# Sink products of two head pairs side by side at half depth, and a new order of the later steps, in a fused attention and gated-MLP kernel

## The chip, the cores and the metric

The kernel runs on one core of a Trainium2 chip. The core has five engines that work at the same time: TensorE (PE, with its weight loads shown as PEld) for matrix products, VectorE (DVE), ScalarE (ACT), GpSimd (POOL), and SyncE (SP), which here issues DMA transfers. Engines wait for one another through semaphores. The metric is the device time of one execution in microseconds; the median of several runs is compared.

## The reference, cut to what matters

```python
def _attn_ref(q, k, v, n_sink, window):          # q, k, v: 4 batches, 8 heads, 768 positions, 64
    scores = np.matmul(q, k.transpose(0, 1, 3, 2)) / np.sqrt(D)
    keep = (pos[None, :] < 4) | in_window         # 4 sink keys, and the last 128 keys
    a = softmax(np.where(keep, scores, -1e9))
    return np.matmul(a, v)

def _moe_ref(x, w_in, g_ln, w_sg, b_sg, w_out):   # x: 4, 768, 512
    u, v = np.split(gelu(x @ w_in), 2, axis=-1)
    v_n = (v - mean) / np.sqrt(var + 1e-6) * g_ln
    v_s = np.einsum('ts,bsd->btd', w_sg, v_n) + b_sg[None, :, None]
    return x + (u * v_s) @ w_out
```

The attention's output, heads laid side by side, is the `x` of the second function.

## The kernel before

The kernel is a list of steps, `STEPS`, written out by hand or by a planner outside the kernel. A loop runs over the list and calls, for each step, the function of that name with the numbers behind it; a last letter A, D or P chooses ScalarE, VectorE or GpSimd. Each engine carries out its own steps in the order of the list. Nothing reorders them. A step on one engine waits only for the steps whose results, or whose freed buffers, it needs.

The numbers are the batch b (0 to 3), then a head pair p (0 to 3; two heads fill 128 partitions), a pair of 128-row token tiles g (0 to 2), a half of the tokens, or a token tile.

- Loads: `LQ.b.i`, `LK.b.i` (a tile of q or k), `LVH.b.i` (v of four heads), `LW`, `LWS`, `LWO`, `LB` (weights). All are issued by POOL, and at most eight are under way: the ninth waits, in POOL's queue, for the first to land.
- Turning q and k so that the head dimension lies on partitions: `TQ`, `TK` on PE and their copies `EQ`, `EK` for batches 0 to 2, DMA transposes `DQ`, `DK` from SP for batch 3.
- Scores: `QK.b.p.g` (PE, two heads on rows 0-63 and 64-127 of the array), `EX` (exponential, ACT), `MK` (window mask: one multiplication on DVE, or two selects on POOL).
- Sink scores of all heads at once: `KS` (DVE), `SK` (PE), `SX` (ACT). They lie in `exs`, 32 partitions for each head pair, so pairs 0 and 1 fill partitions 0-63 and pairs 2 and 3 fill 64-127. `VSM.b` (DVE) makes `v_sink`, the sink rows of v, zero outside each head's own partitions.
- `AV.b.p.k` (PE): products with v for half k of the tokens (three token tiles in batches 1 to 3). For each tile and head one or two products of 65 columns (lines 524 and 528), then for tiles from the third on one sink product of 130 columns over all 128 partitions of `exs` (line 531). `NR` (DVE) divides by the sum and writes `x_sb`.
- Turning x: `XT`/`XE` in batch 0, in the others a DMA transpose `XD.b.half` from SP.
- MLP: `MV`/`GV` (the v half of x @ w_in on PE, gelu on ACT), `BN` (statistics, DVE), `RS` (reciprocal root, POOL), `NM` (DVE), `Z` (normalised v, ACT or DVE); `MU`/`GU` (the u half); `WT`/`WE` turn w_sg once; `SP.b.half.dc` (PE, product with w_sg over all six z tiles of the batch), `GT` (DVE), `GM` (times u, DVE or POOL), `OU.b.t` (PE, output product), `RA` (adds x, DVE), `ST` (store, SP). `OH`, `RH`, `SH` are the same in halves of the columns for the last tile.
- `HM.n` puts n products on a zero tile in front of the next product that takes a fresh buffer. `TBL` touches ACT with an exponential or a gelu.

What couples the engines are rings of buffers: `fresh(ring, key)` takes the next tile of a ring and so waits until the tile's last reader is done. PSUM holds two score tiles (`sc`, for `QK`, `MV`, `MU`) and four others (`mm`, for transposes, `SK`, `AV`, `SP`, `OU`). Ten tiles `P` hold exponentials.

The steps before and after one another in the list are on purpose a mixture of batches: the MLP of batch b runs between the attention steps of batch b+1.

Of the kernel before, what the change touches and what calls it, by code (L numbers as in the profile page):

```python
# [25 lines left out]
MK.0.1.0.D SX.0.1 SX.0.2 QK.0.3.1 MK.0.2.1.P GCP.D NR.0.0.0 EX.0.3.0 AV.0.0.1 AV.0.1.0 AV.0.1.1 NR.0.0.1 EX.0.3.1
QK.0.1.2 NR.0.1.0 AV.0.2.0 AV.0.3.0 EX.0.1.2 MK.0.3.1.P NR.0.1.1 QK.0.2.2 AV.0.2.1 NR.0.2.0 EX.0.2.2 TQ.1.0 NR.0.3.0
MK.0.1.2.P QK.0.3.2 AV.0.3.1 EQ.1.0.A NR.0.2.1 XT.0.0 NR.0.3.1 LWS.0 AV.0.0.2 EX.0.3.2 TBL.G AV.0.1.2 XE.0.0.D LK.1.1
XT.0.1 MK.0.2.2.D MV.0.0 XE.0.1.A LK.1.2 NR.0.0.2 MK.0.3.2.D LK.1.3 NR.0.1.2 AV.0.2.2 AV.0.3.2 LQ.1.2 NR.0.2.2 GV.0.0
MV.0.1 NR.0.3.2 LQ.1.3 BN.0.0 LWS.1 XT.0.2 GV.0.1 MU.0.1 XE.0.2.A BN.0.1 WT.0 GU.0.1 TK.1.0 MV.0.2 RS.0.1 EK.1.0.A  # L30
LK.1.4 NM.0.1 WE.0.A WT.1 GV.0.2 LK.1.5 TK.1.1 MU.0.2 LB.P EK.1.1.A BN.0.2 Z.0.0.A LK.2.0 WT.2 GU.0.2 MU.0.0 WE.1.D
RS.0.2 WE.2.D Z.0.1.A LQ.2.0 NM.0.2 Z.0.2.A Z.0.3.D Z.0.4.D WT.3 LQ.2.1 WT.4 GU.0.0 TBL.E WE.3.D WT.5 LQ.1.4 Z.0.5.D
TQ.1.1 QK.1.0.0 EQ.1.1.D QK.1.1.0 LQ.1.5 SP.0.0.0 WE.4.D LK.2.1 EX.1.0.0 VSM.1 SP.0.0.1 WE.5.D EX.1.1.0 LVH.1.0
GT.0.0.0 TK.1.2 KS.1 GT.0.0.1 QK.1.2.0 QK.1.3.0 EX.1.2.0 SP.0.0.2 LVH.1.1 GM.0.0.0.D EX.1.3.0 MK.1.2.0.D TQ.2.0
EK.1.2.A LQ.2.2 QK.1.0.1 EQ.2.0.D QK.1.1.1 TQ.1.2 EX.1.0.1 GT.0.0.2 LWO SP.0.0.3 EQ.1.2.D EX.1.1.1 LK.2.2 MK.1.0.1.D
TK.2.0 MK.1.0.0.D QK.1.2.1 LK.2.3 EK.2.0.A QK.1.3.1 MK.1.3.0.D SK.1.0 GM.0.0.1.D LQ.2.3 SP.0.1.0 EX.1.2.1 GT.0.0.3
MK.1.1.0.D LQ.2.4 EX.1.3.1 SP.0.1.1 MK.1.1.1.D LQ.2.5 MK.1.2.1.D SX.1.0 QK.1.0.2 QK.1.1.2 GT.0.1.0 EX.1.0.2 GM.0.0.2.P
SP.0.1.2 GT.0.1.1 EX.1.1.2 LK.2.4 GM.0.1.0.D AV.1.0.0 MK.1.3.1.D AV.1.1.0 LK.2.5 GM.0.0.3.D QK.1.2.2 GT.0.1.2 QK.1.3.2
EX.1.2.2 SP.0.1.3 NR.1.0.0 MK.1.1.2.P EX.1.3.2 NR.1.1.0 AV.1.2.0 AV.1.3.0 MK.1.0.2.P GT.0.1.3 QK.2.0.0 QK.2.1.0
NR.1.2.0 EX.2.0.0 OU.0.0 MK.1.2.2.P NR.1.3.0 TK.2.1 RA.0.0 AV.1.0.1 XD.1.0 EK.2.1.A MK.1.3.2.P AV.1.1.1 NR.1.0.1  # L40
AV.1.2.1 EX.2.1.0 GM.0.1.2.P NR.1.1.1 AV.1.3.1 NR.1.2.1 QK.2.2.0 LK.3.0 QK.2.3.0 EX.2.2.0 OU.0.1 NR.1.3.1 GM.0.1.3.P
EX.2.3.0 TBL.G OU.0.2 XD.1.1 RA.0.1 GM.0.1.1.P TK.2.2 MK.2.3.0.D TQ.2.1 LVH.2.0 TQ.2.2 EQ.2.1.D MV.1.0 EQ.2.2.D LQ.3.0
EK.2.2.D LQ.3.1 VSM.2 MU.1.0 GV.1.0 MK.2.1.0.D LVH.2.1 BN.1.0 MV.1.1 GU.1.0 LQ.3.2 RA.0.2 LQ.3.3 MK.2.0.0.D MV.1.2
GV.1.1 MK.2.2.0.D LK.3.1 KS.2 LK.3.2 BN.1.1 MU.1.1 GV.1.2 LK.3.3 BN.1.2 RS.1.1 MU.1.2 GU.1.1 LQ.3.4 NM.1.1 Z.1.0.A
RS.1.2 OU.0.3 GU.1.2 TBL.E LQ.3.5 NM.1.2 Z.1.1.D SK.2.0 Z.1.4.D QK.2.0.1 Z.1.2.D Z.1.3.A QK.2.1.1 Z.1.5.D OU.0.4
# [5 lines left out]
AV.2.2.1 GM.1.1.3.P ST.0.1 NR.2.1.1 AV.2.3.1 ST.0.2 ST.0.5 GM.1.1.0.P SK.3.0 NR.2.2.1 QK.3.2.0 QK.3.3.0 NR.2.3.1
EX.3.2.0 GM.1.1.2.P SP.1.0.2 EX.3.3.0 XD.2.1 SP.1.0.3 GT.1.0.2 SX.3.0 TBL.G MK.3.3.0.D MV.2.0 GM.1.0.2.P DK.3.1
GM.1.1.1.D LK.3.4 MK.3.0.0.D OU.1.3 LVH.3.0 GV.2.0 OU.1.4 RA.1.3 LVH.3.1 OU.1.5 ST.1.3 RA.1.4 GT.1.0.3 MV.2.1 ST.1.4
MK.3.1.0.D LK.3.5 BN.2.0 GM.1.0.3.P MV.2.2 GV.2.1 BN.2.1 MU.2.1 GV.2.2 BN.2.2 RS.2.1 MU.2.0 GU.2.1 NM.2.1 RA.1.5
RS.2.2 MU.2.2 GU.2.0 NM.2.2 Z.2.4.D Z.2.5.D Z.2.0.A Z.2.1.D OU.1.0 GU.2.2 TBL.E Z.2.2.D MK.3.2.0.D OU.1.1 RA.1.0
Z.2.3.D QK.3.0.1 QK.3.1.1 RA.1.1 SP.2.0.0 EX.3.0.1 DK.3.2 EX.3.1.1 OU.1.2 MK.3.0.1.P GT.2.0.0 ST.1.5 VSM.3 ST.1.0
QK.3.2.1 ST.1.1 QK.3.3.1 EX.3.2.1 SP.2.1.0 GM.2.0.0.D MK.3.1.1.P RA.1.2 EX.3.3.1 SP.2.0.1 ST.1.2 MK.3.3.1.P QK.3.0.2
GT.2.0.1 QK.3.1.2 EX.3.0.2 SP.2.1.1 GT.2.1.0 MK.3.2.1.P EX.3.1.2 GM.2.1.0.D SP.2.1.2 GT.2.1.1 GM.2.0.1.D AV.3.0.0
MK.3.1.2.P GT.2.1.2 AV.3.1.0 NR.3.0.0 AV.3.2.0 AV.3.3.0 MK.3.0.2.P NR.3.1.0 QK.3.2.2 QK.3.3.2 EX.3.2.2 SP.2.0.2
NR.3.2.0 NR.3.3.0 EX.3.3.2 TBL.G SP.2.0.3 MK.3.2.2.P GT.2.0.2 XD.3.0 AV.3.0.1 GT.2.0.3 MK.3.3.2.P AV.3.1.1 NR.3.0.1  # L60
# [16 lines left out]
def kernel(  # L77
# [412 lines left out]
    def MK(b, p, g, e="D"):  # L490
        w = wide(g)
        pt = P[b, p, g]
        if e == "D":
# [4 lines left out]
        nc.gpsimd.affine_select(out=p4[:, :, :, 0:128], in_=p4[:, :, :, 0:128], compare_op=ALU.is_ge,  # L498
                                fill=0.0, base=0, pattern=[[0, 2], [0, 2], [1, 128]],
                                channel_multiplier=-1)  # L500
        nc.gpsimd.affine_select(out=p4[:, :, :, 128:256], in_=p4[:, :, :, 128:256],  # L501
                                compare_op=ALU.is_ge, fill=0.0, base=-1,
                                pattern=[[0, 2], [0, 2], [-1, 128]], channel_multiplier=1)
# [7 lines left out]

    def AV(b, p, k):
        vb = v_sb[b]
        fresh(mm_ring, ("a", b, p, k))
        av = av_view(b, p, k)
        i0, n = rowsof(b, k)
        first = True
        for il in range(n):
            i = i0 + il
            for hl in range(2):  # L520
# [5 lines left out]
                if i >= 1:  # L526
                    c = 128 if i % 2 else 384
                    nc.tensor.matmul(av[:, il, hl, :], pt[:, hl, c:c + 128], vb[:, h, i - 1, :],  # L528
                                     start=False, stop=(i < 2 and il == n - 1 and hl == 1))
# [186 lines left out]
```

## Time and profile before

| | |
|---|---|
| runs of the kernel before | median 155.58 us of 3 (155.23 to 155.91) |
| the profiled execution | 155.89 us, of which the span of instructions is 154.2 us |
| instructions | 3867 |
| DVE, ACT, POOL busy | 122.9, 100.0, 99.7 us |
| DMA | 24.67 MB in 87178 packets |

The profile is one execution. Its page gives busy time by engine, the span in 40 slices, and the chain of waits that ended last. The timeline lists instructions in order of time, those of one kind merged, with an idle time in brackets where the engine stood, and what ended it. Shapes are partitions x elements; `64*128` in front of a product is the part of the array that it uses (rows * columns). Times within a row are microseconds from the span's start. Durations of products overlap, since they are pipelined.

### The profile page before, as it was taken

To read this page: it belongs to the slowest core of one execution; us is meant where nothing else is said; L and a number is where in the kernel's file an instruction comes from. 1 tells how busy PE (TensorE), PEld (TensorE's weight loads), DVE (VectorE), ACT (ScalarE), POOL (GpSimd) and SP (SyncE) were. 2 spreads that over 40 slices of the span, in tenths; PEclk is the share of its full clock that TensorE was granted. 3 is DMA by queue.
4 is the path that set the end of the run, shared out by engine and by line. 5 is a ranking of instruction groups with operands and counts; after the bars stand their busy time and mean duration, and the time that the engine had idled before them with its cause. 6 is when DMAs were issued, how large, how long until landed. Compare 5 with 4: busy or idle time off the path is not lost.

```text
span 154.2 us, 3867 instructions
## 1 busy us (share of the span) xinstructions
PE 145.7 (95%) x1540; PEld 94.5 (61%) x1554; DVE 122.9 (80%) x296; ACT 100.0 (65%) x117; POOL 99.7 (65%) x127
## 2 busy tenths in 40 slices
...
PEclk9999999999999999999999999999999999999999
...
DMA packets 87178, 24.67 MB, mean 160 GB/s; under 512 B 78772, under 2 KB 84920, under 8 KB 87160
## 3 DMA queue, kind: packets, MB, share of 16 engines
...
q8 instruction: 12, 0.20, 0.5%
q14 instruction: 6, 0.05, 0.1%
...
## 4 chain that ended last, share of the span: by engine, by line
PE 54%; POOL 18%; DMA 15%; ACT 4%; DVE 4%; issue 2%; SPq 1%; DVEq 0%; ACTq 0%; POOLq 0%
PE mm L627 15%; DMA v_sb<-in_v_dram 11%; PE mm L644 10%; PE sc L566 9%; PE sc L607 8%; POOL q L225 5%; POOL k L225 4%; DMA uT<-in_k_dram 4%; PE sc L483 4%; PE mm L524 3%; POOL v_sb L271 3%; PE mm L528 2%; POOL wsg_gated L637 2%; POOL P L498 2%; POOL P L501 2%
## 5 line engine op out<-in xcount | busy, mean ns | idle before, releaser
L488 ACT ACTIVATE P<-sc 128x1024 bf16<-128x1024 f32 (+1 forms) x48 | 43.4, 952 | 10.3 <-PE sc L483 10.1
L627 PE MATMUL mm<-wsgT,z 128*128 128x384 bf16 x192 | 34.4, 327 | 0.3 <-ACT z L597 0.3
L627 PEld LDWEIGHTS <-z 128*128 128x128 bf16 x192 | 17.6, 98 | 12.5 <-issue 0.7
L570 ACT ACTIVATE vt<-sc 128x1024 f32<-128x1024 f32 x12 | 12.3, 1027 | 18.4 <-PE sc L566 18.4
L632 DVE SCALAR_TENSOR_TENSOR gtmp<-mm,g_sb,b_bc 128x384 bf16<-128x384 f32 x32 | 19.0, 610 | 4.2 <-PE mm L627 4.0
L637 POOL TENSOR_TENSOR wsg_gated<-gtmp,uT 128x384 bf16<-128x384 bf16 x15 | 14.9, 1006 | 11.3 <-DVE gtmp L632 11.2
L607 PE MATMUL sc<-xT,w_in_sb 128*128 128x256 bf16 x192 | 22.1, 273 | 0.0
L566 PE MATMUL sc<-w_in_sb,xT 128*128 128x512 bf16 x92 | 21.8, 379 | 0.2
L644 PE MATMUL mm<-w_out_sb,wsg_gated 128*128 128x512 bf16 x85 | 21.2, 379 | 0.5
L498 POOL TENSOR_SCALAR_AFFINE_SELECT P<-P 128x512 bf16<-128x512 bf16 x21 | 13.7, 653 | 11.4 <-ACT P L488 11.4
L607 PEld LDWEIGHTS <-w_in_sb 128*128 128x128 bf16 x192 | 18.7, 98 | 2.9
L579 DVE BATCH_NORM_STATS2 st<-vt 128x6 f32<-128x512 f32 x24 | 15.4, 685 | 6.1 <-ACT vt L570 6.0
L541 DVE TENSOR_TENSOR x_sb<-mm,rcp 128x384 bf16<-128x384 f32 (+1 forms) x36 | 18.5, 513 | 1.2
L588 POOL TENSOR_TENSOR rs<-rs,neg_half 128x4 f32<-128x4 f32 (+1 forms) x8 | 7.1, 882 | 15.8 <-DVE rs L583 14.4
L225 POOL DMA_DIRECT2D k<-in_k_dram x18 | 16.4, 924 | 1.3 <-DMA v_sb<-in_v_dram 1.3
L648 DVE TENSOR_TENSOR ot<-mm,x_sb 128x512 f32<-128x512 f32 x23 | 15.4, 683 | 2.2 <-PE mm L644 2.2
L225 POOL DMA_DIRECT2D q<-in_q_dram x18 | 16.8, 956 | 0.0
L524 PE MATMUL mm<-v_sb,P 128*128 128x65 bf16 x192 | 16.1, 194 | 0.6 <-DVE x_sb L541 0.4
L524 PEld LDWEIGHTS <-P 128*128 128x128 bf16 x192 | 14.5, 97 | 2.5 <-DMA v_sb<-in_v_dram 0.6
L528 PE MATMUL mm<-v_sb,P 128*128 128x65 bf16 x160 | 15.4, 193 | 0.4 <-POOL P L501 0.4
L612 ACT ACTIVATE uT<-sc 128x1024 bf16<-128x1024 f32 x12 | 12.2, 1024 | 5.1 <-PE sc L607 5.1
L566 PEld LDWEIGHTS <-xT 128*128 128x128 bf16 x96 | 9.2, 98 | 10.1
...
## 6 DMA issues: line engine op xcount, KB each, us to landing
...
```

Source lines behind the costliest of these rows:

```text
L225: return nc.gpsimd.dma_start(out=dst.rearrange("p (h d) -> p h d", h=H), in_=heads(src, b, i))
L488: nc.scalar.activation(out=P.new((b, p, g))[:, :, 0:w], in_=sc_ring[b, p, g][:, :, 0:w], func=AF.Exp, scale=scale)
L498: nc.gpsimd.affine_select(out=p4[:, :, :, 0:128], in_=p4[:, :, :, 0:128], compare_op=ALU.is_ge, fill=0.0, base=0, pattern=[[0, 2], [0, 2], ...
L524: nc.tensor.matmul(av[:, il, hl, :], pt[:, hl, c:c + 128], vb[:, h, i, :], start=first, stop=False)
L528: nc.tensor.matmul(av[:, il, hl, :], pt[:, hl, c:c + 128], vb[:, h, i - 1, :], start=False, stop=(i < 2 and il == n - 1 and hl == 1))
L541: nc.vector.tensor_mul(x_sb.get(b)[:, i0:i0 + n, 128 * p:128 * (p + 1)].rearrange("p t (h d) -> p t h d", h=2), av[:, :, :, 0:Dh], rcp[:, ...
L566: nc.tensor.matmul(hp[:, jl, :], xT[b][:, 2 * g + jl, c, :], w_in_sb[:, c, d_half:2 * d_half], start=(c == 0), stop=(c == KD - 1))
L607: nc.tensor.matmul(hp[:, dc // 2, 256 * (dc % 2):256 * (dc % 2 + 1)], w_in_sb[:, c, 128 * dc:128 * (dc + 1)], xT[b][:, 2 * g:2 * g + 2, c, :],
L627: nc.tensor.matmul(ps[:, 0:NH], z[b][:, si, 128 * dc:128 * (dc + 1)], wsgT[:, si, NH * hf:NH * (hf + 1)], start=(si == 0), stop=(si == NT ...
L632: nc.vector.scalar_tensor_tensor(out=gtmp.new((b, hf, dc)), in0=mm_ring["g", b, hf, dc][:, 0:NH], scalar=g_sb[:, dc:dc + 1], in1=b_bc[:, N ...
L637: (nc.vector if e == "D" else nc.gpsimd).tensor_mul(gated(b, hf)[:, dc, :], gtmp[b, hf, dc], uT[b][:, dc, NH * hf:NH * (hf + 1)])
L644: nc.tensor.matmul(ps, gated(b, hf)[:, dc, 128 * tl:128 * (tl + 1)], w_out_sb[:, dc, :], start=(dc == 0), stop=(dc == KU - 1))
```

## The change

In batches 1 and 2, for the second half of the tokens, `AV` no longer issues its sink products. A new step `SN.b.p0.k` issues them for head pairs p0 and p0 + 2 together, ahead of their `AV`: for each of the three token tiles one product on partitions 0-63 (pair p0) and one on 64-127 (pair p0 + 2), each into its own accumulator. `SN` takes both `mm` tiles, opens the accumulation, and `AV` adds to it. Batches 0 and 3 keep the old products.

The first 145 steps of the list that issue work stay as they are. (Steps `MK...N` are new in the list there and issue nothing.) From then on the list is in another order: the score steps `QK` stand in other pairs and more often alone; some copies, masks, multiplications and `Z` steps change between ACT, DVE and POOL; loads stand at other places among POOL's masks; `HM.2` and `HM.1` are new in front of `WT.2` and `WT.3`; `TBL` steps stand elsewhere, and two more of them end the list's ACT part.

```diff
+    def split(b, k):
+        return k == 1 and b in (1, 2)
+
+    def SN(b, p0, k):
+        i0, n = rowsof(b, k)
+        for p in (p0, p0 + 2):
+            fresh(mm_ring, ("a", b, p, k))
+        for il in range(n):
+            for p in (p0, p0 + 2):
+                rows = slice(64 * (p // 2), 64 * (p // 2) + 64)
+                nc.tensor.matmul(av_view(b, p, k)[:, il, :, :].rearrange("p h d -> p (h d)"),
+                                 exs[b][rows, 128 * (i0 + il - 2):128 * (i0 + il - 1)],
+                                 v_sink[b][rows, 2 * p:2 * p + 2, :].rearrange("p h d -> p (h d)"),
+                                 start=(il == 0), stop=False)
+
     def AV(b, p, k):
         vb = v_sb[b]
-        fresh(mm_ring, ("a", b, p, k))
+        if not split(b, k):
+            fresh(mm_ring, ("a", b, p, k))
...
-        first = True
+        first = not split(b, k)
...
-                                     start=False, stop=(i < 2 and il == n - 1 and hl == 1))
-            if i >= 2:
+                                     start=False,
+                                     stop=((i < 2 or split(b, k)) and il == n - 1 and hl == 1))
+            if i >= 2 and not split(b, k):
...
```

The list from the place where the orders part up to batch 1's `MV.1.0`, before:

```text
LK.1.4 NM.0.1 WE.0.A WT.1 GV.0.2 LK.1.5 TK.1.1 MU.0.2 LB.P EK.1.1.A BN.0.2 Z.0.0.A LK.2.0 WT.2 GU.0.2 MU.0.0 WE.1.D
RS.0.2 WE.2.D Z.0.1.A LQ.2.0 NM.0.2 Z.0.2.A Z.0.3.D Z.0.4.D WT.3 LQ.2.1 WT.4 GU.0.0 TBL.E WE.3.D WT.5 LQ.1.4 Z.0.5.D
TQ.1.1 QK.1.0.0 EQ.1.1.D QK.1.1.0 LQ.1.5 SP.0.0.0 WE.4.D LK.2.1 EX.1.0.0 VSM.1 SP.0.0.1 WE.5.D EX.1.1.0 LVH.1.0
...
SP.0.1.2 GT.0.1.1 EX.1.1.2 LK.2.4 GM.0.1.0.D AV.1.0.0 MK.1.3.1.D AV.1.1.0 LK.2.5 GM.0.0.3.D QK.1.2.2 GT.0.1.2 QK.1.3.2
EX.1.2.2 SP.0.1.3 NR.1.0.0 MK.1.1.2.P EX.1.3.2 NR.1.1.0 AV.1.2.0 AV.1.3.0 MK.1.0.2.P GT.0.1.3 QK.2.0.0 QK.2.1.0
NR.1.2.0 EX.2.0.0 OU.0.0 MK.1.2.2.P NR.1.3.0 TK.2.1 RA.0.0 AV.1.0.1 XD.1.0 EK.2.1.A MK.1.3.2.P AV.1.1.1 NR.1.0.1
AV.1.2.1 EX.2.1.0 GM.0.1.2.P NR.1.1.1 AV.1.3.1 NR.1.2.1 QK.2.2.0 LK.3.0 QK.2.3.0 EX.2.2.0 OU.0.1 NR.1.3.1 GM.0.1.3.P
EX.2.3.0 TBL.G OU.0.2 XD.1.1 RA.0.1 GM.0.1.1.P TK.2.2 MK.2.3.0.D TQ.2.1 LVH.2.0 TQ.2.2 EQ.2.1.D MV.1.0
```

and after:

```text
LK.1.4 MU.0.2 RS.0.1 LK.1.5 WE.0.A HM.2 WT.2 LB.P NM.0.1 EK.1.0.A GV.0.2 Z.0.2.D GU.0.2 LK.2.0
BN.0.2 LQ.2.0 Z.0.1.D TK.1.1 TQ.1.1 RS.0.2 EK.1.1.D LQ.2.1 Z.0.0.A Z.0.3.A MU.0.0 WT.1 WE.2.D WT.4 NM.0.2 Z.0.4.A KS.1
EQ.1.1.D WE.1.D WT.5 Z.0.5.D WE.4.D TK.1.2 WE.5.D VSM.1 LQ.1.4 QK.1.1.0 EK.1.2.D GU.0.0 LQ.1.5 EX.1.1.0 QK.1.0.0
...
SP.0.1.3 EX.1.3.1 EK.2.0.D QK.1.2.2 QK.1.1.2 MK.1.2.1.D GT.0.1.3 MK.1.0.1.P AV.1.0.0 GM.0.0.3.P LQ.2.4 GT.0.1.0 LQ.2.5
NR.1.0.0 LK.2.4 SP.0.1.2 MK.1.3.1.P EX.1.2.2 LK.2.5 AV.1.2.0 MK.1.2.2.P QK.1.3.2 MK.1.0.2.D AV.1.3.0 EX.1.1.2 GT.0.1.2
QK.2.1.0 EX.1.3.2 EX.2.1.0 OU.0.0 MK.1.3.2.P NR.1.2.0 TK.2.1 QK.2.0.0 NR.1.3.0 MK.1.1.2.P SN.1.0.1 RA.0.0 AV.1.0.1
TQ.2.1 XD.1.0 EK.2.1.A AV.1.2.1 QK.2.3.0 NR.1.0.1 SN.1.1.1 NR.1.2.1 EQ.2.1.A EX.2.0.0 AV.1.1.1 AV.1.3.1 OU.0.1
QK.2.2.0 TQ.2.2 LK.3.0 NR.1.1.1 GM.0.1.3.P NR.1.3.1 GM.0.1.2.P EX.2.3.0 TK.2.2 OU.0.2 RA.0.1 MV.1.0
```

Around batch 1's second product with w_sg and batch 2's attention, after:

```text
BN.1.2 LQ.3.4 GU.1.1 OU.0.4 OU.0.3 NM.1.1 Z.1.2.D LQ.3.5 QK.2.0.1 Z.1.1.A Z.1.3.D RS.1.2 RA.0.4 Z.1.0.D GU.1.2 EX.2.0.1 NM.1.2
Z.1.4.D Z.1.5.D QK.2.1.1 EX.2.1.1 DK.3.0 SK.2.0 RA.0.3 SP.1.1.0
...
QK.2.3.2 QK.2.2.2 OU.0.5 EX.2.2.2 SP.1.1.3 MK.2.1.2.P RA.0.5 EX.2.3.2 ST.0.4 SN.2.0.1 QK.3.1.0 XD.2.0 QK.3.0.0
GT.1.1.3 EX.3.1.0 ST.0.1 AV.2.0.1 MK.2.2.2.P AV.2.2.1 ST.0.2 SN.2.1.1 MK.2.3.2.P QK.3.3.0 NR.2.0.1 AV.2.1.1
...
OU.1.3 GT.1.0.2 KS.3 GM.1.0.2.P XD.2.1 DK.3.1 SK.3.0 MK.3.3.0.D SX.3.0 LK.3.4 QK.3.2.0 LVH.3.0 LVH.3.1 EX.3.2.0 MV.2.0
```

More of the change, by code (lines that the diff above doesn't have):

```diff
@@ L26 @@
[L26 to L45, printed above, removed]
@@ L51 @@
[L51 to L60, printed above, removed]
@@ new lines @@
+LQ.3.2 EK.2.2.A MV.1.1 MK.2.2.0.D MV.1.2 MK.2.1.0.D GV.1.1 LQ.3.3 LK.3.1 KS.2 TBL.G.2 LK.3.2 LK.3.3 BN.1.0 GV.1.2
+MU.1.1 GM.0.1.0.D BN.1.1 RS.1.1 MU.1.2 BN.1.2 LQ.3.4 GU.1.1 OU.0.4 OU.0.3 NM.1.1 Z.1.2.D LQ.3.5 QK.2.0.1 Z.1.1.A
+Z.1.3.D RS.1.2 RA.0.4 Z.1.0.D GU.1.2 EX.2.0.1 NM.1.2 Z.1.4.D Z.1.5.D QK.2.1.1 EX.2.1.1 DK.3.0 SK.2.0 RA.0.3 SP.1.1.0
+SP.1.0.1 QK.2.3.1 SX.2.0 GT.1.1.0 QK.2.2.1 GM.1.1.0.D MK.2.0.1.D EX.2.2.1 DQ.3.0 MK.2.1.1.P ST.0.3 EX.2.3.1 GT.1.0.1
+MK.2.2.1.P SP.1.1.2 DQ.3.1 MK.2.3.1.P SP.1.0.0 GM.1.0.1.D AV.2.0.0 QK.2.1.2 QK.2.0.2 GT.1.1.2 NR.2.0.0 GT.1.0.0
```

68 lines of the change are left out of this document (48 added, 20 removed).

## The prediction

> **What bounds the kernel now.** I read the page first, then TensorE's timeline step by step, then the waits that the timeline names.
>
> ```profile
> span 154.2 us, 3867 instructions
> ...
> PE 145.7 (95%) x1540; PEld 94.5 (61%) x1554; DVE 122.9 (80%) x296; ACT 100.0 (65%) x117; POOL 99.7 (65%) x127
> ...
> PEclk9999999999999999999999999999999999999999
> ...
> PE 54%; POOL 18%; DMA 15%; ACT 4%; DVE 4%; issue 2%; SPq 1%; DVEq 0%; ACTq 0%; POOLq 0%
> ```
>
> TensorE (PE) is busy for 95% of the span at the full granted clock, and the chain that ended last runs through it more than through anything else. So a product costs its place in line: the distance from its start to the start of the next step. I therefore price by starts, not by durations. In the timeline below the columns are start, duration, engine, line, operation, operands, shapes and count:
>
> ```profile
> 32.32 0.50 PE L619 MATMUL mm<-iden,wsg_gated 128*128 128x128 bf16 x6
> ...
> 37.93 0.61 PE L382 MATMUL mm<-iden,q 128*128 128x128 bf16 x8
> 38.48 0.50 PE L483 MATMUL sc<-qT,kT 64*128 64x256 bf16 x8
> 38.91 2.12 PE L627 MATMUL mm<-wsgT,z 128*128 128x384 bf16 x12
> 40.87 0.61 PE L382 MATMUL mm<-iden,k 128*128 128x128 bf16 x8
> ...
> 48.84 0.61 PE L483 MATMUL sc<-qT,kT 64*128 64x256 bf16 x12
> 49.38 1.15 PE L627 MATMUL mm<-wsgT,z 128*128 128x384 bf16 x6
> ...
> 61.11 0.61 PE L382 MATMUL mm<-iden,k 128*128 128x128 bf16 x8
> 61.56 1.06 PE L382 MATMUL mm<-iden,q 128*128 128x128 bf16 x16
> 62.45 1.89 PE L566 MATMUL sc<-w_in_sb,xT 128*128 128x512 bf16 x8
> 64.18 1.91 PE L607 MATMUL sc<-xT,w_in_sb 128*128 128x256 bf16 x16
> ```
>
> Three prices come out. Eight transposes followed by more of their kind take 61.56 - 61.11 = 0.45 us; in front of score products (64 rows) the same eight take 38.48 - 37.93 = 0.55. So **entering half-depth work costs 0.10**. The two score steps at 48.84 stream 2 x (2 x 256 + 4 x 128) = 2048 columns and take 0.54. At L627's pace (12 x 384 columns in 1.96 us) these would take 0.87 one after the other, and half of that side by side: 0.44, plus **0.10 for leaving**. So products on rows 0-63 and 64-127 overlap here. And a 512-column product costs (64.18 - 62.45) / 8 = 0.216.
>
> TensorE does stop in a few places:
>
> ```profile
> 53.54 0.50 PE L483 MATMUL sc<-qT,kT 64*128 64x256 bf16 x8
> ...
> 55.07 0.39 PE L382 MATMUL mm<-iden,k 128*128 128x128 bf16 x4
> 55.83 0.40 PE L382 MATMUL mm<-iden,k 128*128 128x128 bf16 x4 [0.37 <-DMA k<-in_k_dram]
> 56.06 0.19 PE L524 MATMUL mm<-v_sb,P 128*128 128x65 bf16 x1
> ...
> 57.92 0.20 PE L524 MATMUL mm<-v_sb,P 128*128 128x65 bf16 x1
> 58.51 0.20 PE L528 MATMUL mm<-v_sb,P 128*128 128x65 bf16 x1 [0.39 <-POOL P L501]
> ...
> 75.65 0.76 PE L627 MATMUL mm<-wsgT,z 128*128 128x384 bf16 x3
> 76.67 1.15 PE L627 MATMUL mm<-wsgT,z 128*128 128x384 bf16 x6 [0.26 <-ACT z L597]
> ...
> 88.06 0.22 PE L531 MATMUL mm<-v_sink,exs 128*128 128x130 bf16 x1
> 88.34 0.20 PE L524 MATMUL mm<-v_sb,P 128*128 128x65 bf16 x1
> ```
>
> Measured against the prices: from 53.54 to 55.07 stand 0.43 of scores and 0.86 of OU.0.0 (four 512-column products), so 0.24 is lost; TK.2.1 takes 0.99 for 0.45, 0.54 lost; AV.1.3.1 stands 0.59 - 0.03 = 0.56 for a Pool mask; SP.1.0.0 needs 0.49 for three products and takes 1.02, 0.53 lost on z; the gap after 88.06 is 0.28 for 0.06, 0.22 lost. Together **2.1 us** of waiting between 32.3 us and the end. That is all a new order can take away from TensorE, and the work it adds must come out of it.
>
> **The change, part by part.**
>
> *Sink products.* In batches 1 and 2, 24 full-depth products of 130 columns go; 24 half-depth ones in 12 side-by-side pairs come.
>
> ```profile
> 25.84 0.22 PE L531 MATMUL mm<-v_sink,exs 128*128 128x130 bf16 x1
> 25.89 0.38 PE L566 MATMUL sc<-w_in_sb,xT 128*128 128x512 bf16 x1
> ...
> L531 PEld LDWEIGHTS <-exs 128*128 128x128 bf16 x64 | 6.2, 98 | 0.0
> ```
>
> A full one costs 0.05 to 0.06. No row shows a half-depth sink pair. Below, it cannot be cheaper than one such product (0.06); above, two weight loads one after the other, 0.196. I take 0.06, since the score products (other weights for each, same 64 rows) do overlap. 24 x 0.06 - 12 x 0.06 = **-0.7 us**. SN holds two accumulators at once, so it waits for two NR steps; behind it on TensorE wait the AV products and the next scores. By my count the later NR ends 0.1 to 0.6 before.
> The Trainium skill, TensorE: Matmul & The Clock Gate, Back-to-back issue gap, gives about 81 ns a product for a stream of weight load and 128-column product. By it the 24 half products would take 1.9 us and the sum be 1.2 us longer; the transposes above, each with its own weight load, stand 56 ns apart (0.45 / 8), so the trace disagrees and the row decides.
>
> *Switches.* The new order takes the score steps apart: from the 145 kept steps on, half-depth work stood in 18 groups and stands in 23, and SK in the midst of one adds its own. Counting changes of shape along TensorE's order: 39 before, 49 after, at 0.10: **+1.0 us**, eight of the ten extra ones in front of MV.1.0. SN itself shares a group with scores and adds none.
>
> *Warm products.* HM.2 and HM.1 put three 512-column products in front of WT.2 and WT.3: **+0.65**. The clock is at full already and I find no wait there that they could fill.
>
> So the work grows by 1.0 us, and the question is which waits are left. I follow TensorE's new order by the prices above and set each producer's list beside it.
>
> *Stretch 1, 32.3 to MV.1.0 (62.45 before).* Before: 30.1 us, 1.35 of it waits (the first three), so 28.8 of work. After: +0.85 switches, +0.65 warm, -0.35 sinks = 29.9. The three waits had two sources, Pool's list and the loads:
>
> ```profile
> 36.08 3.81 POOL L225 DMA_DIRECT2D q<-in_q_dram  x4
> ...
> 51.85 1.82 POOL L225 DMA_DIRECT2D k<-in_k_dram  x2 [1.32 <-DMA v_sb<-in_v_dram]
> 53.67 0.67 POOL L498 TENSOR_SCALAR_AFFINE_SELECT P<-P 128x512 bf16<-128x512 bf16 x1
> ...
> 58.43 0.90 POOL L637 TENSOR_TENSOR wsg_gated<-gtmp,uT 128x384 bf16<-128x384 bf16 x1
> ...
> 73.26 0.76 POOL L588 TENSOR_TENSOR rs<-rs,neg_half 128x2 f32<-128x2 f32 x1
> ```
>
> Pool's last mask of this batch ended at 58.43. Its new list up to MK.1.1.2.P has one load less (LQ.2.0 goes ahead of RS.0.2, -0.95), one multiplication (+0.9) and one mask more ((58.43 - 53.67) / 4 = 1.19), and puts masks where it stood 1.32 for a v load: 58.43 - 0.95 + 0.9 + 1.19 - 1.32 = 58.25. TensorE stands at AV.1.1.1 at 58.5 (3.7 ahead of MV.1.0: two AV halves, one score group, two OU, two transposes) and needs that mask 0.1 later. Cover 0.4. The loads go out about a place earlier and are asked for as late or later, so their waits go too. Small misses (SN on NR.1.3.0, a mask slowed by DVE): 0.3. The stretch gives **0 to +0.1**: the waits are bought out with work.
>
> *Stretch 2, the first products of batch 1's MLP.* Same work. MV.1.1 needs the transposed half sent by XD.1.1:
>
> ```profile
> DMA to landing us min/median/max: 3.7/4.4/5.2
> ...
> 59.34 0.56 DVE L541 TENSOR_TENSOR x_sb<-mm,rcp 128x384 bf16<-128x384 f32 x1
> ...
> 74.13 2.35 DVE L600 TENSOR_SCALAR z<-vt,rs,nmr 128x512 bf16<-128x512 f32 x4
> ```
>
> Before, the last NR ended at 59.9 and MV.1.1 began at 65.93 (64.18 + 1.75): 6.0 of room. After, AV.1.3.1 ends near 59.3 and its NR, queued fourth on DVE, at 60.5: 5.2 of room against a landing of 3.7 to 5.2. I book **+0.25** (0 to 0.6).
>
> *Stretch 3, to MV.2.0 (92.06 before).* Equal work but for SN (-0.35) and two switches (+0.2). SP.1.1.0's wait for z: Z steps cost 2.35 / 4 = 0.59 on DVE. RS.1.2 ends near 74.1 although LQ.3.5 now stands ahead of it on Pool, since LQ.3.5's 0.95 replaces lateness Pool no longer has; two Z after it end at 75.9, and TensorE, at SP.1.1.0 by about 76.0, asks for z's last tile 0.8 later: gone, -0.53. The wait after 88.06 (a DVE mask) is a Pool mask with 0.5 of cover now: -0.22. New near misses: SP.1.1.3 on NR.2.3.0, QK.3.1.0 on EX.2.3.2, 0.2 of cover each; I book +0.2. **-0.7.**
>
> *Stretch 4, to the end.* The same steps in nearly the same pairs. LK.3.5 goes out later, behind GM.1.0.3.P and RS.2.2, and on SP DK.3.2 after it, with the stores ST.1.5 and ST.1.0 to ST.1.2 behind. By my count it still lands about 1 us ahead of QK.3.0.2, which uses it; any lateness past that is a wait of TensorE. No one waits for those stores. TBL moves and swaps of copies, masks and multiplications among ACT, DVE and Pool cost nothing while TensorE's line covers them: ACT and Pool are busy 65%. The last two table loads fall where ACT is done. **0.**
>
> ```profile
> 149.47 1.04 PE L657 MATMUL mm<-w_out_sb,wsg_gated 128*128 128x256 bf16 x8
> ```
>
> The tail from this last product (0.9 of it) to the span's end, addition and store, stays.
>
> Sum on the profiled span: work +1.0, old waits -2.1, new waits +0.7 (0.3, 0.25, 0.2): **-0.4**. The profiled execution took 155.89, a little over the median 155.58; -0.4 from the median is **155.2**.
>
> **The rivals.**
>
> *Every cover holds.* No new wait: -1.1, 154.5. For it: most waits fall away by whole tenths. Against: five covers are under 0.3, thinner than one contended mask.
>
> *Pool runs late (slower).* The masks of batch 1 now stand between the loads. If LK.2.4 again stands for a v load (1.32) and a mask is slowed by DVE as here,
>
> ```profile
> 109.45 1.09 POOL L501 TENSOR_SCALAR_AFFINE_SELECT P<-P 128x512 bf16<-128x512 bf16 x1
> ```
>
> (1.09 instead of 0.6 for one half of a mask), MK.1.1.2.P comes late. From 0.4 of lateness on, each us is a us of TensorE. The wait and two slowed halves make 2.3, 1.9 past the cover, in place of the 0.3 booked: -0.4 - 0.3 + 1.9 = +1.2, 156.8. Against: that v load had landed by 51.85, and Pool reaches LK.2.4 only near 52.
>
> *The pairs do not overlap.* The change would not do what it says: +0.7 at 0.06 each (155.9), +1.65 at a weight load each. Against: L483.
>
> **How the numbers follow.** Forecast 155.2 (its own range 154.8 to 155.9) 0.46; every cover holds 0.24; Pool late 0.22; no overlap 0.08. Half a per cent, 0.8 us, is about what a measurement of this kernel can tell from no change. Faster than 154.8: the second case and a little of the first, 0.28. Slower than 156.36: the third and part of the fourth, 0.26. Within: 0.46. The range takes in the good end and Pool's price: 154.4 to 156.8.
>
> **What would show it.** Right: SN's six products take about 0.2 from first start to the next step; single score steps cost 0.1 on each side; MV.1.0 begins within 0.3 of 62.45 and MV.2.0 about 0.4 ahead of 92.9 (92.06 and OU.1.3's 0.86, which now comes first). Wrong: a wait over 0.5 at AV.1.1.1 for Pool, at MV.1.1 or MV.2.1 for xT, or in the last 60 us, where I book none; or SN taking 0.35 and more.

## The result, and the profile after

The changed kernel took 154.99 us (median of 22 runs, 154.32 to 156.17) against 155.84 us for the kernel before beside it (22 runs): a ratio of 0.9947, interval 0.9924 to 0.997. The forecast was 155.2 within 154.4 to 156.8. Direction and range held; the gain was about twice the 0.4 us forecast.

The page of the changed kernel, the lines that answer to those shown of before:

```profile
span 153.2 us, 3868 instructions
...
PE 146.7 (96%) x1542; PEld 94.3 (62%) x1557; DVE 122.6 (80%) x295; ACT 103.7 (68%) x120; POOL 98.8 (64%) x127
...
PEclk9999999999999999999999999999999999999999
...
PE 86%; DMA 9%; issue 1%; DVE 1%; SPq 1%; POOL 1%; DVEq 0%
```

TensorE has 1 us more of busy time in a span that is 1 us shorter. The chain that ended last, which was 54% TensorE, 18% Pool and 15% DMA, is now 86% TensorE: Pool and a part of the loads have left it. What is left to see is TensorE's own timeline (start, duration, engine, line, operation, shapes, count; L191 is a warm product, L525 `SN`, L543 and L547 `AV`, L484 `QK`, L586 `MV`, L677 `OH`):

```profile
32.46 1.91 PE L627 MATMUL sc<-xT,w_in_sb 128*128 128x256 bf16 x16
...
34.21 0.59 PE L191 MATMUL mm<-warm 128*128 128x512 bf16 x2
34.64 0.50 PE L639 MATMUL mm<-iden,wsg_gated 128*128 128x128 bf16 x6
...
56.62 0.58 PE L525 MATMUL mm<-v_sink,exs 64*128 64x130 bf16 x6
57.14 0.20 PE L543 MATMUL mm<-v_sb,P 128*128 128x65 bf16 x1
...
58.60 0.33 PE L525 MATMUL mm<-v_sink,exs 64*128 64x130 bf16 x6
58.87 0.20 PE L543 MATMUL mm<-v_sb,P 128*128 128x65 bf16 x1
...
62.61 1.89 PE L586 MATMUL sc<-w_in_sb,xT 128*128 128x512 bf16 x8
...
85.96 0.34 PE L525 MATMUL mm<-v_sink,exs 64*128 64x130 bf16 x6
86.14 0.49 PE L484 MATMUL sc<-qT,kT 64*128 64x256 bf16 x8
...
92.10 0.39 PE L586 MATMUL sc<-w_in_sb,xT 128*128 128x512 bf16 x1
...
148.57 1.04 PE L677 MATMUL mm<-w_out_sb,wsg_gated 128*128 128x256 bf16 x8
```

Read by starts, as the prediction did. The distance from the start of a step to the start of the next is called its slot here; cover is the time by which a result is ready ahead of the product that needs it. The slot of `SN.2.0.1` is 86.14 - 85.96 = 0.18 for six products. `SN.1.1.1` takes 58.87 - 58.60 = 0.27, with the 0.10 for leaving half depth. `SN.1.0.1` takes 57.14 - 56.62 = 0.52 for the same work: **0.25 of waiting, and the only wait of any size on TensorE from 32.46 to the last product**. None stands at AV.1.1.1 (58.87), MV.1.1, MV.2.0 or in the last 60 us.

Every other slot of the changed kernel lies within 0.03 of those of its kind. Counted in this way, the kernel before waited 2.3 us, a little more than the 2.1 of the prediction: AV.1.3.1 lost 0.63 rather than 0.56, and two pairs of score steps take 0.62 and 0.63, where the pair at 48.84 takes 0.54:

```profile
74.16 0.69 PE L483 MATMUL sc<-qT,kT 64*128 64x256 bf16 x12
...
109.39 0.70 PE L483 MATMUL sc<-qT,kT 64*128 64x256 bf16 x12
```

The yardstick for all that follows is the distance from the first step after the kept part (WT.1 at 32.32 before, MU.0.2 at 32.46 after; the same step, MV.0.2, ends just ahead of both) to OH.3.5.0. Before it is 149.47 - 32.32 = 117.15, after 148.57 - 32.46 = 116.11: **-1.04 us**. By stretches: to MV.1.0 +0.02; to MV.2.0 -0.98 (OU.1.3's 0.86, which moved ahead of it, taken out); to the end -0.08.

### The profile page after: what moved, and what is told of

The parts are those of the page before. It is cut to its first block, busy times and chain, and to the rows that moved or that the text cites. A ratio compares the mean times of both kernels' runs of the same rounds, so it can differ in the third digit from the quotient of the medians.

```text
span 153.2 us, 3868 instructions
## 1 busy us (share of the span) xinstructions
PE 146.7 (96%) x1542; PEld 94.3 (62%) x1557; DVE 122.6 (80%) x295; ACT 103.7 (68%) x120; POOL 98.8 (64%) x127
## 4 chain that ended last, share of the span: by engine, by line
PE 86%; DMA 9%; issue 1%; DVE 1%; SPq 1%; POOL 1%; DVEq 0%
PE mm L647 21%; PE sc L627 14%; PE sc L586 13%; PE mm L664 13%; PE sc L484 7%; DMA v_sb<-in_v_dram 5%; PE mm L543 5%; DMA uT<-in_k_dram 4%; PE mm L383 4%; PE mm L547 3%; PE mm L551 1%; PE mm L639 1%; PE mm L570 1%; PE mm L525 1%; PE mm L463 1%
## 5 line engine op out<-in xcount | busy, mean ns | idle before, releaser
L586 PE MATMUL sc<-w_in_sb,xT 128*128 128x512 bf16 x93 | 21.9, 379 | 0.2
L657 POOL TENSOR_TENSOR wsg_gated<-gtmp,uT 128x384 bf16<-128x384 bf16 x15 | 14.2, 958 | 11.1 <-DVE gtmp L652 11.0
L561 DVE TENSOR_TENSOR x_sb<-mm,rcp 128x384 bf16<-128x384 f32 (+1 forms) x36 | 18.5, 513 | 1.2
L608 POOL TENSOR_TENSOR rs<-rs,neg_half 128x4 f32<-128x4 f32 (+1 forms) x8 | 7.6, 953 | 16.5 <-DVE rs L603 15.7
L543 PE MATMUL mm<-v_sb,P 128*128 128x65 bf16 x192 | 15.3, 194 | 0.5 <-DVE x_sb L561 0.4
L484 PE MATMUL sc<-qT,kT 64*128 64x128 bf16 (+1 forms) x256 | 15.4, 238 | 0.2
L586 PEld LDWEIGHTS <-xT 128*128 128x128 bf16 x96 | 9.2, 98 | 10.3 <-issue 0.2
L543 PEld LDWEIGHTS <-P 128*128 128x128 bf16 x192 | 13.4, 98 | 2.9 <-DMA v_sb<-in_v_dram 0.6
```

Of the source, the lines that this page charges most:

```text
L484: nc.tensor.matmul(sc[:, hl, c:c + 128 * ni], at(kT, b)[rows, j, p, :], at(qT, b)[rows, i:i + ni, p, :], start=not biased, stop=(not biase ...
L561: nc.vector.tensor_mul(x_sb.get(b)[:, i0:i0 + n, 128 * p:128 * (p + 1)].rearrange("p t (h d) -> p t h d", h=2), av[:, :, :, 0:Dh], rcp[:, ...
L586: nc.tensor.matmul(hp[:, jl, :], xT[b][:, 2 * g + jl, c, :], w_in_sb[:, c, d_half:2 * d_half], start=(c == 0), stop=(c == KD - 1))
```

## Experiments

Each profiled execution gives that distance; the kernel before was traced once, the changed kernel twice (e12). "Against changed" is its difference to 116.11; it is free of what happens in the first 32 us, which the times are not. The three groups of four ran on three chips, each beside the kernel before (medians 156.09, 155.63 and 155.90).

| kernel | MU.0.2 to OH.3.5.0 | distance | against changed | median us | ratio to before, interval |
|---|---|---|---|---|---|
| before | 32.32 (WT.1), 149.47 | 117.15 | +1.04 | 155.84 | |
| changed | 32.46, 148.57 | 116.11 | | 154.99 | 0.9947, 0.9924 to 0.997 |
| e1 full sinks | 32.46, 149.15 | 116.69 | +0.58 | 155.91 | 0.9999, 0.9971 to 1.0028 |
| e2 no warm products | 33.38, 149.94 | 116.56 | +0.45 | 155.89 | 0.9983, 0.9955 to 1.0011 |
| e3 sinks in turn | 32.70, 148.81 | 116.11 | 0.00 | 154.97 | 0.9941, 0.9899 to 0.9982 |
| e4 Pool late | 32.83, 149.59 | 116.76 | +0.65 | 156.13 | 1.0007, 0.9976 to 1.0039 |
| e5 no HM.1 | 32.51, 148.50 | 115.99 | -0.12 | 155.11 | 0.9969, 0.9938 to 1.0 |
| e6 copy on ACT | 33.24, 149.49 | 116.25 | +0.14 | 155.65 | 0.9993, 0.9961 to 1.0025 |
| e7 mask moved | 32.89, 149.07 | 116.18 | +0.07 | 155.44 | 0.9985, 0.9951 to 1.002 |
| e8 all edits | 32.15, 149.12 | 116.97 | +0.86 | 156.39 | 1.0051, 1.0023 to 1.0078 |
| e9 mask early | 32.25, 148.11 | 115.86 | -0.25 | 155.12 | 0.9963, 0.9933 to 0.9994 |
| e10 mask early, no HM.1 | 33.87, 151.65 | 117.78 | +1.67 | 157.25 | 1.0101, 1.0058 to 1.0144 |
| e11 groups split | 31.89, 148.73 | 116.84 | +0.73 | 156.12 | 1.0015, 0.998 to 1.005 |
| e12 changed again | 33.03, 149.14 | 116.11 | 0.00 | 155.69 | 0.9995, 0.9966 to 1.0025 |

### What the sink pairs are worth: e1, e3

```diff
     def split(b, k):
-        return k == 1 and b in (1, 2)
+        return False
```

> The new order kept, the sink products of batches 1 and 2 at full depth inside AV again; SN issues nothing. Theory (a pair costs one product of 0.06, and the pairs are worth 24 x 0.06 - 12 x 0.06 = 0.7, less SN.1.0.1's measured wait of 0.23): AV.b.p.1 takes 0.53 instead of 0.36 in batches 1 and 2, no wait stands at 56.6, and the time is 0.4 to 0.5 us above the changed kernel's (155.4). Rival (the gain is all the order's, a pair saves nothing or the freed time becomes a wait elsewhere): within 0.15 us of the changed kernel.

Measured +0.58, more than either end of the theory. The AV slots of the two batches grow by 0.17 each, eight times, and the work of the four SN steps goes: +1.36 - 0.70 = +0.66. SN.1.0.1's wait goes too, -0.25. Of the remaining 0.17, 0.15 is a wait that SN had hidden. The kernel with full sinks first (TensorE, then ACT), the changed kernel second, at the end of SP.1.1.3:

```profile
84.98 1.14 PE L649 MATMUL mm<-wsgT,z 128*128 128x384 bf16 x6
86.20 0.29 PE L484 MATMUL sc<-qT,kT 64*128 64x256 bf16 x2
...
84.21 1.94 ACT L489 ACTIVATE P<-sc 128x1024 bf16<-128x1024 f32 x2 [1.00 <-PE sc L484]
```

```profile
84.89 1.14 PE L647 MATMUL mm<-wsgT,z 128*128 128x384 bf16 x6
85.96 0.34 PE L525 MATMUL mm<-v_sink,exs 64*128 64x130 bf16 x6
86.14 0.27 PE L484 MATMUL sc<-qT,kT 64*128 64x256 bf16 x2
```

Without SN, QK.3.1.0 starts 1.22 after the SP step instead of 1.07. It needs the score tile that EX.2.3.2, the second of the two exponentials, reads until 86.15, and starts at 86.20: the near miss that I had booked as a wait. In the changed kernel SN.2.0.1 stands in it. So the pairs carry 0.58 of the 1.04, and the order with the warm products the other 0.46.

```diff
-        for il in range(n):
-            for p in (p0, p0 + 2):
+        for p in (p0, p0 + 2):
+            for il in range(n):
```

> SN issues three products on rows 0 to 63 and then three on rows 64 to 127, instead of alternating. Theory (side by side needs neighbours on different rows): each SN has only one neighbouring pair on different rows, so its six products take 5 x 0.06 = 0.30 (0.27 to 0.36) instead of 0.18: four of them +0.4 to +0.6 us in all, though at SN.1.0.1 part of it lies in the wait that stands there. Rival (the order within SN does not matter): 0.18 each and no difference in time.

The rival held: no difference at all. SN.2.0.1 in this kernel:

```profile
86.19 0.35 PE L525 MATMUL mm<-v_sink,exs 64*128 64x130 bf16 x6
86.37 0.50 PE L484 MATMUL sc<-qT,kT 64*128 64x256 bf16 x8
```

Three products on rows 0-63 issued ahead of three on rows 64-127 still take 0.18. In SN.1.1.1 of this trace the six starts stand in three couples (58.828 and 58.831, 58.885 and 58.888, 58.941 and 58.945). The trace does not name the rows of a product, but SN.1.0.1 shows that the order of issue did change: three products start at 56.858, 56.915 and 56.971, and the other three, which wait for NR.1.3.0, at 57.109, 57.165 and 57.220; in the changed kernel one alone starts ahead of that wait. So the two halves run beside each other whatever the order of issue, at least over six products.

### What a wait of Pool's would have cost: e4

```diff
-MK.1.3.2.P NR.1.2.0 TK.2.1
+MK.1.3.2.P MK.1.3.2.P NR.1.2.0 TK.2.1
```

> One mask of Pool's list (MK.1.3.2.P) issued twice, so that the masks behind it come 1.19 us later; the second time it changes nothing in the data. Theory (Pool's cover at AV.1.1.1 is 0.5 in the changed kernel: MK.1.1.2.P ends at 58.46 and is needed by the fifth product at 59.00): a wait of 0.6 to 0.75 for Pool appears inside AV.1.1.1, and the time rises by the same 0.6 to 0.75. Rival (the lateness is lost in other slack, or Pool is further ahead than its row says): no wait at AV.1.1.1 and less than 0.2 us.

Pool's end of MK.1.1.2.P, and AV.1.1.1 on TensorE:

```profile
59.35 0.63 POOL L504 TENSOR_SCALAR_AFFINE_SELECT P<-P 128x512 bf16<-128x512 bf16 x1
```

```profile
59.23 0.20 PE L543 MATMUL mm<-v_sb,P 128*128 128x65 bf16 x1
...
60.04 0.20 PE L547 MATMUL mm<-v_sb,P 128*128 128x65 bf16 x1 [0.38 <-POOL P L504]
```

AV.1.1.1 takes 1.035 instead of 0.378, and all of the 0.66 reaches the end (+0.65). The mask ends at 59.98 and the products go on at 60.04. So Pool's cover was 1.19 - 0.66 = 0.53, where the prediction had 0.4, and past it each us is a us: the mechanism and price of the slower rival were real, its lateness did not come.

### What the warm products do: e2, e5, e7, e8

```diff
-HM.2 WT.2 LB.P
+WT.2 LB.P
...
-EX.1.0.0 HM.1 WT.3
+EX.1.0.0 WT.3
```

> The three warm products HM.2 and HM.1 of the changed stretch left out, all else as in the changed kernel. Theory (they are work on TensorE with nothing to fill): TensorE is 0.65 ahead at QK.1.3.0 (41.23 in the changed kernel), granted clock unchanged, and 0.3 to 0.65 of it reaches the end (154.3 to 154.7), the rest going into thin covers: Pool's mask for AV.1.1.1 (0.5 of cover) and SN.1.0.1's wait for NR.1.3.0. Rival (they fill time in which TensorE would stand, or hold the clock up): a wait or a slower stretch of the same length appears before MV.1.0, and the time stays within 0.15 us of the changed kernel or rises.

The rival held, by the first of its two reasons: the kernel is 0.45 slower without them, at the same full clock. Two waits appear on TensorE:

```profile
41.94 0.34 PE L484 MATMUL sc<-qT,kT 64*128 64x256 bf16 x4 [0.37 <-ACT P L489]
...
49.65 0.20 PE L543 MATMUL mm<-v_sb,P 128*128 128x65 bf16 x1 [0.49 <-DVE P L498]
```

QK.1.3.0 loses 0.43 on EX.1.1.0: ACT's list up to it (a GU, the table load, the exponentials) does not start earlier because TensorE does. AV.1.1.0 loses 0.66 on the mask MK.1.1.1.D. Two masks ahead of that one, in DVE's timeline of this kernel and then of the changed one:

```profile
46.55 1.92 DVE L498 TENSOR_TENSOR P<-P,mask 128x768 bf16<-128x768 bf16 x2
```

```profile
45.58 1.46 DVE L498 TENSOR_TENSOR P<-P,mask 128x768 bf16<-128x768 bf16 x2
```

The pair took 0.46 longer here, in a place without cover. In both kernels Pool only issues loads beside these masks, but at other moments of them. Why a load's issue slows a mask at one moment and not at another stays open.

Leaving out HM.1 alone:

> Only the single warm product HM.1 left out, HM.2 kept. The run without all three showed TensorE 0.43 late at QK.1.3.0 for EX.1.1.0 and 0.66 late at AV.1.1.0 for the mask MK.1.1.1.D on DVE, in an execution whose start was itself 0.9 later. Theory (the warm products stand in waiting time: in the changed kernel EX.1.1.0 ends 0.2 to 0.3 ahead of QK.1.3.0 and MK.1.1.1.D has no cover at AV.1.1.0): 0.2 is gained at QK.1.3.0 and given back, with up to 0.66 more, at AV.1.1.0; counted from MU.0.2 the end is 0 to 0.5 us later than the changed kernel's. Rival (the losses of that run came from its late start): counted from MU.0.2 the end is 0.21 earlier and AV.1.1.0 waits for nothing.

Measured -0.12: 0.21 gained, 0.095 given back at AV.1.1.0. Neither reading fully held. The wait is there, for MK.1.1.1.D has only 0.12 of cover at AV.1.1.0; the further 0.57 of e2 is not, and the two masks took 1.46 here, as in the changed kernel.

```diff
-SK.1.0 MK.1.3.0.D GT.0.0.3 SP.0.1.1
+SK.1.0 GT.0.0.3 SP.0.1.1
...
-MK.1.1.1.D AV.1.1.0 NR.1.1.0 TK.2.0
+MK.1.1.1.D AV.1.1.0 NR.1.1.0 MK.1.3.0.D TK.2.0
```

> All three warm products left out as before, and one DVE mask that is not needed until AV.1.3.0 (MK.1.3.0.D) put behind MK.1.1.1.D. Theory (without the warm products AV.1.1.0 waits for DVE's queue, and QK.1.3.0 for ACT): the 0.43 at QK.1.3.0 stays, the 0.66 at AV.1.1.0 goes, and counted from MU.0.2 the end is 0.1 to 0.25 us earlier than the changed kernel's. Rival (AV.1.1.0's wait has another source, or the later mask is late in its turn): a wait of 0.3 or more at AV.1.1.0 or AV.1.3.0, and no gain.

AV.1.1.0's wait went and the 0.43 at QK.1.3.0 stayed, as the theory had it; but SP.0.1.2 now stood 0.21 longer, and the end was +0.07. With every remedy together (this edit, the copy of e6, and SP.0.0.1 ahead of QK.1.3.0):

> The two former edits together, and SP.0.0.1 put ahead of QK.1.3.0, so that EX.1.1.0 has 1 us more. Theory (each wait has the one source named): QK.1.3.0, AV.1.1.0 and SN.1.0.1 all start without a wait, and of 0.65 + 0.23 at least 0.5 reaches the end; the rest goes to Pool's list at AV.1.1.1, whose cover of 0.5 is used up, and to xT at MV.1.1, which landed 0.27 ahead. Time 154.1 to 154.5. Rival (TensorE is held by the other engines' lists as much as by its own, so that each wait moved shows up at the next step): within 0.2 us of the changed kernel.

The rival held, and worse: +0.86. TensorE reached AV.1.1.0 0.64 earlier against its own start, and then waited 0.52 there, 0.80 in front of SP.0.1.3 and 0.43 in MV.1.1, for a mask, for a GT behind a slow mask, and for xT:

```profile
47.85 0.20 PE L543 MATMUL mm<-v_sb,P 128*128 128x65 bf16 x1 [0.35 <-DVE P L498]
...
50.91 0.81 PE L647 MATMUL mm<-wsgT,z 128*128 128x384 bf16 x4 [0.64 <-DVE gtmp L652]
...
67.49 0.82 PE L586 MATMUL sc<-w_in_sb,xT 128*128 128x512 bf16 x3 [0.26 <-DMA xT<-x_sb]
```

Each of these waits ends with another engine's work. How little room the other engines have there is seen in the busy times of three stretches of the changed kernel (from:to, length, then busy us and count of PE, PEld, DVE, ACT, POOL, then the clock and two figures of DMA that are not used here):

```profile
32.50:44.70 12.20, 12.20 (x142) 9.47 (x141) 10.29 (x23) 10.36 (x14) 11.79 (x14) 1.00 2.01 182
44.70:57.40 12.70, 12.61 (x170) 8.12 (x169) 11.98 (x23) 10.73 (x14) 12.70 (x18) 1.00 2.43 163
57.40:149.00 91.60, 91.13 (x855) 57.68 (x861) 75.84 (x178) 56.22 (x64) 51.41 (x63) 1.00 0.99 138
```

From 44.7 to 57.4 Pool is busy for all of 12.70 us and DVE for 11.98: with TensorE, three engines are full or nearly so at once. After 57.4 there is room again, on Pool above all. That this is the reason in general is argued from these times; no run frees Pool or DVE alone.

### The one wait that was left: e6, e9, e10

DVE of the changed kernel ahead of SN.1.0.1, which needs the end of NR.1.3.0 (L560, L561):

```profile
53.54 1.37 DVE L498 TENSOR_TENSOR P<-P,mask 128x1024 bf16<-128x1024 bf16 x1
54.83 0.60 DVE L652 SCALAR_TENSOR_TENSOR gtmp<-mm,g_sb,b_bc 128x384 bf16<-128x384 f32 x1
55.36 0.18 DVE L560 RECIPROCAL rcp<-mm 128x6 f32<-128x6 f32 x1
55.58 0.56 DVE L561 TENSOR_TENSOR x_sb<-mm,rcp 128x384 bf16<-128x384 f32 x1
56.05 0.19 DVE L560 RECIPROCAL rcp<-mm 128x6 f32<-128x6 f32 x1
56.27 0.56 DVE L561 TENSOR_TENSOR x_sb<-mm,rcp 128x384 bf16<-128x384 f32 x1
```

```diff
-EX.1.3.1 EK.2.0.D QK.1.2.2
+EX.1.3.1 EK.2.0.A QK.1.2.2
```

> One copy (EK.2.0, 0.68 on DVE) given to ACT, where gaps of 0.4 to 0.7 stand. Theory (SN.1.0.1's wait of 0.23 is DVE's list: busy without a gap from 49.4 to 57.4, NR.1.3.0 ends 0.2 late): NR.1.3.0 comes 0.68 earlier, SN.1.0.1 takes 0.29 instead of 0.52, and MV.1.0 and the end come 0.2 earlier. Rival (the copy on ACT, 1.0 long, makes SP.0.1.2, which needs its buffer at 52.53, or the next exponentials late by as much): no gain, or up to 0.3 slower.

No gain, and by neither reason given: DVE stood 0.61 for TensorE in the freed place, the same mask then took 1.51, and the wait grew by 0.14. The length of the list was not the source. The slowed mask is left as the likely one, and the next run tries it.

```diff
-MK.1.2.1.D GT.0.1.3 MK.1.0.1.P
+MK.1.2.1.D MK.1.0.2.D GT.0.1.3 MK.1.0.1.P
...
-QK.1.3.2 MK.1.0.2.D AV.1.3.0
+QK.1.3.2 AV.1.3.0
```

> The copy on ACT again, and the mask MK.1.0.2.D put ahead of GT.0.1.3, where the former run showed DVE standing 0.61 for TensorE; behind it the mask had taken 1.51 instead of 0.68 beside Pool's. Theory (SN.1.0.1's wait is this slowed mask in DVE's list): NR.1.3.0 comes 0.8 or more earlier, SN.1.0.1 takes 0.29, MV.1.0 and the end are 0.2 earlier counted from MU.0.2, unless MV.1.1, whose xT had 0.27 of cover, takes it back. Rival (the mask is slowed at the new place too, or the GT steps behind it hold AV.1.2.0): the wait moves to AV.1.2.0 or stays, no gain.

The theory held. DVE, then TensorE, of this kernel:

```profile
49.75 1.80 DVE L498 TENSOR_TENSOR P<-P,mask 128x768 bf16<-128x768 bf16 x3
...
55.04 0.56 DVE L561 TENSOR_TENSOR x_sb<-mm,rcp 128x384 bf16<-128x384 f32 x1
```

```profile
56.41 0.33 PE L525 MATMUL mm<-v_sink,exs 64*128 64x130 bf16 x6
56.68 0.20 PE L543 MATMUL mm<-v_sb,P 128*128 128x65 bf16 x1
```

The three masks take 0.60 each on the average, NR.1.3.0 ends at 55.60, and SN.1.0.1 takes 0.27: its wait of 0.25 is gone, and the 0.25 reaches the end. By its trace this kernel beats both; by its times it beats the kernel before narrowly (0.9963), and its median of 155.12 stands against 155.69 for the changed kernel on the same chip.

The same with HM.1 out and MK.1.3.0.D moved:

> The same, with HM.1 left out and MK.1.3.0.D behind MK.1.1.1.D. Theory (HM.1's 0.21 was given back at AV.1.1.0 and SP.0.1.2 only for DVE's list): QK.1.3.0 starts 0.17 to 0.21 earlier, no wait at AV.1.1.0 nor SP.0.1.2, and the end is 0.4 earlier counted from MU.0.2 (154.6 where the changed kernel has 155.0). Rival: DVE's or ACT's list gives the wait at the next step that asks, and the end is within 0.15 of the changed kernel's.

The rival held, far beyond its size: +1.67, with 0.79 and 0.92 lost for GT steps and 0.43 for xT. The same three masks in this kernel:

```profile
52.40 2.91 DVE L498 TENSOR_TENSOR P<-P,mask 128x768 bf16<-128x768 bf16 x3
```

That is 0.97 each on the average instead of 0.60, and the mask before them took 1.31.

### The price of a change of shape, and the changed kernel again: e11, e12

```diff
-AV.2.0.0 QK.2.1.2 QK.2.0.2 GT.1.1.2 NR.2.0.0 GT.1.0.0 EX.2.1.2 SP.1.1.1
+AV.2.0.0 QK.2.1.2 GT.1.1.2 NR.2.0.0 GT.1.0.0 EX.2.1.2 SP.1.1.1 QK.2.0.2
...
-QK.3.1.1 QK.3.3.1 EX.3.1.1 ST.1.0 RA.1.2 SP.2.0.0
+QK.3.1.1 EX.3.1.1 ST.1.0 RA.1.2 SP.2.0.0 QK.3.3.1
...
-QK.3.0.2 QK.3.1.2 MK.3.3.1.P SP.2.1.2
+QK.3.0.2 MK.3.3.1.P SP.2.1.2 QK.3.1.2
```

> Three pairs of score steps of the second half (QK.2.1.2 and QK.2.0.2, QK.3.1.1 and QK.3.3.1, QK.3.0.2 and QK.3.1.2) taken apart by one SP step each: six more changes of shape and no other work. Theory (0.10 each way): the slots of the steps around grow by 6 x 0.106 = 0.63 in all, TensorE ends 0.6 later counted from MU.0.2, and the time is 0.4 per cent above the changed kernel's. Rival (a change of shape is hidden behind the weight loads of the next step, or the steps only looked longer): less than 0.2.

The theory held. The first of the three places:

```profile
80.17 0.40 PE L484 MATMUL sc<-qT,kT 64*128 64x256 bf16 x6
80.50 1.15 PE L647 MATMUL mm<-wsgT,z 128*128 128x384 bf16 x6
81.58 0.39 PE L484 MATMUL sc<-qT,kT 64*128 64x256 bf16 x6
```

A score step of 0.23 takes 0.33 and the SP step 1.08 instead of 0.98. All six slots grew by 0.095 to 0.097, 0.58 together; a further 0.09 is at AV.2.2.1, and its cause is open. The times (1.0015 against 0.9995) are too coarse to show a difference of this size. A change of shape costs 0.10 us each way. The Trainium skill, TensorEngine Tiling (Array Packing), Key Properties, says that a change of tiling mode drains TensorE and that tiles run independently of each other. The traces agree with both, with 0.10 at a change here and with products of the two halves 3 ns apart in e3.

> The changed kernel again, on the same chip as the three above. Theory and rivals alike: the ratio to the kernel before is 0.9947 within its interval of 0.9924 to 0.997, and TensorE's steps stand where they stood to 0.01 us from MU.0.2 on, so that slots of different runs can be compared.

The slots held to 0.01 us: 116.11 again. The ratio did not: its interval reaches just into the first one's. The difference of the two profiled executions, 155.54 against 154.98, lies wholly ahead of MU.0.2 (33.03 against 32.46).

## Why the prediction was right, and where it fell short

- **Work.** Booked +1.0 (sinks -0.7, switches +1.0, warm +0.65), and that is what came. With the waits taken off, the distance is 117.15 - 2.3 before and 116.11 - 0.25 after: 1.0 more. It holds by stretches too: +1.15 to MV.1.0, -0.13 to MV.2.0 and 0.01 behind it, where +1.15, -0.15 and 0 were booked. So each price held: a pair 0.06, a switch 0.10, warm products 0.43 and 0.21. The count of 49 switches includes those out of SK, whose results lie 32 rows high:

```profile
46.78 0.40 PE L463 MATMUL mm<-qT,ks_sink 128*32 128x512 bf16 x4
47.12 1.15 PE L647 MATMUL mm<-wsgT,z 128*128 128x384 bf16 x6
```

  Its four products start within 0.01 us of one another and run beside each other. One of 512 columns costs 0.216, so 0.11 of the slot of 0.33 (three times before, three times after) is again the price of a change.
- **Old waits, -2.1.** All gone, as forecast. They were 2.3, since small ones had been passed over.
- **New waits, +0.7: the term that was mis-sized.** Measured 0.25. Of stretch 1's 0.3, SN on NR.1.3.0 is the 0.25, at the step and for the releaser named. The 0.25 at MV.1.1 and the 0.2 at the score steps did not come. That is 0.45 of the 0.64 between -0.4 and -1.04; the 0.2 of old waits that I had not counted is the rest.
- **MV.1.1 (stretch 2).** The step that failed: I asked for the second transposed half at MV.1.1's start, while only its fifth product, on the fourth token tile, reads it.

```profile
61.02 1.44 SPq L577 DMA_TRANSPOSE xT<-x_sb  x1
...
DMA to landing us min/median/max: 3.7/4.7/5.6
```

  It left at 61.02 and, with the longest landing, was there at 66.6; needed was 66.08 + 4 x 0.216 = 66.94. The fifth product comes 0.86 later than the start that I reckoned with. Against that the half left at 61.02 instead of 60.5 and landed in 5.6 instead of at most 5.2. The errors nearly cancel, and 0.3 of cover is left: that no wait came is luck, not foresight. In e8, where the landing took 6.3, a wait of 0.43 did come.
- **Score steps (stretch 3).** QK.3.1.0's cover was as thin as booked. What I missed is that SN.2.0.1 stands right in front of it: e1 shows 0.15 of wait there without SN. That SN fills this wait is luck too.
- **Warm products.** Priced rightly, read wrongly. "I find no wait there that they could fill" is what e2 contradicts: they stand where TensorE would wait 0.43 for ACT, and with them two of DVE's masks took 0.46 less. Taking all three out costs 0.45; taking out HM.1 alone gained 0.12 in one trace (e5).
- **The rivals.** "Every cover holds" (-1.1, 154.5) is nearer to the trace than my forecast. One cover failed, by 0.25, and others held by 0.3 (MV.1.1) or 0.5 (Pool). Pool's lateness was a sound mechanism (e4) that did not occur. That the pairs do not overlap is refuted by SN's 0.18.
- **Half a per cent.** I called this what a measurement can tell. The first ratio lies just past it, the second (e12) within it. The traces say -1.04 us, 0.67% of the span, for the part that was changed; for the changed kernel that distance was found twice, for the kernel before once.
